# Retention feeding a channel mix on one core: the same words in a new written order

## The chip, the cores and the metric

The kernel runs on one core of a Trainium2 chip. A core has a matrix engine (TensorE, PE in the profile, with its weight loads as PEld), VectorE (DVE), ScalarE (ACT), GpSimd (POOL, which here only issues loads) and SyncE (SP, which here issues loads and stores). Each works through its own instructions in their written order, and waits on semaphores for the others. PSUM, which takes what PE computes, has eight banks of 512 f32 in each partition. The metric is the device time of one execution in microseconds.

## The reference

Inputs: q, k, v of 4 batches x 8 heads x 768 tokens x 64, two mixing vectors, and weights w_k (512 x 1024), w_v (1024 x 512), w_r (512 x 512), all f32. The output is 4 x 768 x 512 f32.

```python
gamma = 1.0 - 2.0 ** (-5.0 - np.arange(H))
for t in range(S):
    state = gamma * state + outer(k[:, :, t], v[:, :, t])
    y[:, :, t] = (1 / sqrt(D)) * (q[:, :, t] @ state)
x = y with the heads side by side            # batch, token, 512
xk = mu_k * x + (1 - mu_k) * x_prev          # x_prev: the token before
xr = mu_r * x + (1 - mu_r) * x_prev
out = sigmoid(xr @ w_r) * (maximum(xk @ w_k, 0) ** 2 @ w_v)
```

## The kernel before

The 4 x 768 tokens are cut into 12 blocks n of 256 tokens, three to a batch. Within a block the retention is computed in parallel: scores of k against q, masked, times v, plus what the carried state gives; between blocks of a batch the state is carried. Each block then goes through the channel mix. Some blocks are mixed in pairs (GROUPS, line 19: 3 with 4, 6 with 7, 9 with 10). Block 0 is loaded and transposed in two halves of heads.

What is issued, and in which order on every engine, is a written list of words, ORDER (lines 23 to 75). The loop in lines 720 to 734 reads it from the front, and each word calls one function (CODES, line 709), which issues that word's instructions. So the order on each engine is the order of its words in the list. A word is a code, its numbers (the first is nearly always the block n), an engine after ~ where that is open (v DVE, a ACT, p POOL, s SP), and after @ the PSUM bank or pair of banks. Waits between engines come from the data, the buffers and the banks that words share. The words:

| word | what it does | engine, line |
|---|---|---|
| lq, lk, lv | load q, k, v of a block; numbers behind n: a range of head pairs; two loads for k and v of a block from 1 on | POOL or SP, 223 to 238 |
| cq, ck | f32 to f16 of the halves of block 0 that SP loaded into k2s | ACT, 246 |
| wk.h, wv.h, wr | load halves of w_k, w_v; w_r | POOL, 698 to 707 |
| Tq, Tk then Eq, Ek | transposes; their copies out of PSUM | PE 265; ACT 286, 298 |
| vs | v times its decay | DVE 253 |
| S then M | scores; causal mask | PE 313, 325; DVE 346 |
| C, U, G | products for the state; their sums; decay to the next block | PE 360, 374; DVE or ACT 407, 422 |
| I, J, Y | carried state times q, and masked scores times v | PE 433 to 496 |
| D, dx | scaled result into xT; its difference to the token before | DVE 502, 526 |
| X.n.w.j | mix, w = 0 for xk and 1 for xr, j one of four parts; n is the first of its group | DVE 535 |
| K.n.g, Qa, Qb | xk @ w_k, part g; relu; square into k2s | PE 548; ACT 569, 574 |
| R.n.tb, s | xr @ w_r for half tb of the block; sigmoid | PE 589; ACT 598 |
| V.n.tb.half, O, st | product with w_v in two halves; times the sigmoid; store | PE 603; DVE 610; SP 616 |
| Vc, Oc, sc | the same for the last 128 tokens, in two column halves | PE 620; DVE 628; SP or ACT 635 |
| z.c | products of zeros on PE, whose results nobody reads: c // 4 products of f32 and c % 4 of f16, 512 columns each | PE 665 |
| mu, mt, me | load, transpose and copy the mixing vectors | ACT 653, PE 659, ACT 662 |
| gy | powers of the decay | DVE or ACT 681 |

K needs all four X of its block or group with w = 0, R all four with w = 1. Buffers are rings: four each for q, k, v as loaded (Q16, K16, V32), the sigmoids (RS) and the outputs (OS, two a block); three for vs, the transposed q and k, the mixes (XM) and the squares (k2s, whose second and third parts also take the first loads by SP, line 216); two for dx. A word that writes a bank waits until the words that read its last content are done.

The loop that reads the list:

```python
for word in ORDER.split():
    word, _, at = word.partition("@")
    word, _, eng = word.partition("~")
    code, *args = word.split(".")
    ...
    CODES[code](ENG.get(eng), *args)
```

Of the kernel before, what the change touches and what calls it, by code (L numbers as in the profile page):

```python
# [36 lines left out]
Eq.4~a wv.0~p K.2.2@2 Qa.2.2 M.3.1~v K.2.0@3 Qa.2.0 G.3~a M.3.0~v K.2.3@1 vs.4~v Qb.0.3 S.4.1@45
S.4.0@67 M.4.0~v I.3@23 M.4.1~v Qa.2.3 lq.6~p lq.7~p K.2.1@0 Qb.2.0 Y.3 C.4@67 V.1.0.0@1 U.4.0
U.4.1 G.4~a I.4@45 J.3 Qa.2.1 D.3~v dx.3~v Y.4 V.1.1.0@6 Tq.7@23 J.4 D.4~v wv.1~p Qb.2.1
V.0.1.0@0 lk.6~p V.0.0.0@7 X.2.1.2 dx.4~v X.3.0.1 X.3.0.2 X.3.0.3 Eq.7~a V.1.1.1 X.3.0.0 V.0.0.1  # L40
O.0.0 Tk.6@45 Ek.6~a lq.5~p Tq.6@23 lv.5~p Qb.2.2 V.0.1.1 Eq.6~a V.1.0.1 O.1.0 K.3.6@4 K.3.1@5
Qb.2.3 lk.5~p K.3.0@7 Qa.3.6 Tq.5@4 Qa.3.1 Qa.3.0 vs.5~v C.5@5 X.2.1.1 Eq.5~a Tk.5@1 Ek.5~a
S.6@23 O.0.1 O.1.1 lk.7~p U.5.0 Tk.7@67 Ek.7~a X.2.1.0 I.5@45 M.6~v X.3.1.3 K.3.2@0 K.3.3@1
Qa.3.2 Qb.3.1 lv.6~p S.5.0@23 Qa.3.3 Qb.3.0 X.3.1.1 S.5.1@67 Qb.3.3 X.2.1.3 Qb.3.2 K.3.4@0
st.0.0 Qa.3.4 M.5.1~v lk.8~p K.3.5@1 Qa.3.5 R.2.1@6 lv.8~p lk.9~p s.2.1 M.5.0~v Y.5 S.7@23
Tk.8@01 Ek.8~a J.5 X.3.1.0 X.3.1.2 R.3.1@7 s.3.1 V.2.0.0@6 K.3.7@0 lv.7~p vs.6~v R.2.0@7 V.2.0.1
D.5~v M.7~v s.2.0 dx.5~v X.5.1.1 O.2.0 Qa.3.7 Qb.3.6 V.2.1.0@1 Tk.9@23 C.6@45 U.6.0~a Ek.9~a
lq.8~p Tq.8@67 Qb.3.7 X.5.0.3 V.2.1.1 vs.7~v R.4.0@0 Eq.8~a U.6.1 U.6.2 X.5.0.0 U.6.3 st.0.1
R.3.0@2 C.7@45 X.5.0.1 s.4.0 I.6@67 s.3.0 st.1.1 X.5.0.2 K.5.3@3 Qa.5.3 O.2.1 lq.10~p K.5.1@0
Qa.5.1 G.6~v X.5.1.3 V.3.0.0@1 U.7.0 U.7.1 U.7.2 st.2.1 I.7@23 Y.6 vs.8~v U.7.3 G.7~a lq.11~p  # L50
R.4.1@0 D.6~v V.4.1.0@4 lv.11~p C.8@67 Y.7 V.3.1.0@5 Qb.5.1 Qb.3.4 Qb.3.5 V.3.0.1 dx.6~v s.4.1
U.8.0 U.8.1 V.3.1.1 Qb.5.3 D.7~v U.8.2 V.4.1.1 dx.7~v X.6.0.1 X.6.0.3 V.4.0.0@7 K.5.0@6 X.5.1.2
X.6.0.2 Qa.5.0 V.4.0.1 Qb.5.0 K.5.2@0 X.6.0.0 Qa.5.2 Qb.5.2 X.6.1.2 lv.9~p K.6.7@6 Qa.6.7 st.2.0
st.1.0 O.4.1 O.3.0 K.6.0@2 Qa.6.0 lk.10~p O.4.0 O.3.1 st.3.1 K.6.4@0 S.8@67 I.8@23 Tk.10@45
Qa.6.4 K.6.1@1 Ek.10~a X.6.1.1 X.5.1.0 Qa.6.1 Qb.6.1 K.6.6@0 Qb.6.0 Qa.6.6 vs.9~v K.6.5@4 Qa.6.5
M.8~v R.5.1@1 Qb.6.6 Tq.10@67 Eq.10~a s.5.1 Y.8 Tq.11@45 Qb.6.7 lv.10~p vs.10~v X.6.1.3 Eq.11~a
D.8~v dx.8~v lq.9~p X.8.0.2 X.8.0.1 lk.11~p R.5.0@0 s.5.0 K.6.3@6 Qa.6.3 V.5.1.0@7 Tq.9@23
X.6.1.0 Eq.9~a S.10@45 M.10~v Qb.6.3 C.9@01 U.9.0~v st.3.0 U.9.1 V.5.1.1 K.6.2@6 Qa.6.2 R.6.1@2
s.6.1 U.9.2 R.6.0@3 s.6.0 I.9@45 U.9.3 O.5.1 X.8.0.3 S.9@01 M.9~v X.8.0.0 G.9~a C.10@67 U.10.0
U.10.1 Qb.6.2 vs.11~v R.7.1@2 s.7.1 V.5.0.0@3 Qb.6.5 st.4.1 Tk.11@01 Ek.11~a U.10.2 U.10.3  # L60
V.5.0.1 Qb.6.4 K.8.0@2 Qa.8.0 G.10~v I.10@01 Y.9 C.11@67 st.4.0 R.7.0@2 O.5.0 V.6.1.0@3 D.9~v
U.11.0 U.11.1 s.7.0 K.8.3@4 Qa.8.3 V.6.1.1 U.11.2 I.11@67 st.5.0 dx.9~v O.6.1 S.11@45 X.8.1.2
Y.10 V.7.1.0@2 M.11~v D.10~v dx.10~v X.9.0.3 X.9.0.2 X.9.0.1 V.7.0.0@3 Y.11 X.9.0.0 Qb.8.0
# [12 lines left out]


# [687 lines left out]
```

## Time and profile before

| what | us |
|---|---|
| time, median of 3 runs | 156.48 (156.37 to 156.81) |
| the profiled execution's own time | 156.1 |
| its span, first to last instruction | 154.3 |
| PE busy / weight loads busy | 147.3 / 84.2 |
| DVE busy | 128.1 |
| ACT busy | 99.1 |
| POOL busy (issuing loads) | 55.2 |
| granted TensorE clock | 1.000 |

Between the profiled span and the time lie 1.8 us that no instruction covers. A busy share is the share of the span in which an engine had an instruction; matmuls overlap one another and are drawn longer than the distance at which they follow, so PE's share is an upper bound. A group's row gives the line, the engine, the operation, output and inputs by their names, the shape, the count, the busy time, the mean duration, and the idle time before it with what ended it. The lists below speak of words: since each engine runs its words in written order and the number of instructions of each word is known, the instructions of the timeline can be counted off against the list.

### The profile page before, as it was taken

The page shows a single profiled execution, that of the slowest core. Times are in us where ns is not written, and L with a number is a line of the kernel's source. Part 1 is how long each engine was busy: PE and PEld are TensorE (multiplying, and loading weights), DVE is VectorE, ACT ScalarE, POOL GpSimd, SP SyncE. Part 2 cuts the span into 40 slices and gives each one's busy share as a digit, 9 for nine tenths or more (in the row PEclk, how much of TensorE's full clock was granted, in tenths as well). Part 3 has the DMA queues.
Part 4 walks back from the last instruction along what each step waited for, and adds up shares of the span by engine and source line. Part 5 has one row for each costly group of instructions (what it writes and reads, how often), then busy time and mean ns, then how long its engine had stood idle before and what let it go on. Part 6 is the DMA issues. An engine that isn't in the chain of part 4 may idle for free.

```text
span 154.3 us, 5316 instructions
## 1 busy us (share of the span) xinstructions
PE 147.3 (95%) x2316; PEld 84.2 (55%) x2316; DVE 128.1 (83%) x203; ACT 99.1 (64%) x182; POOL 55.2 (36%) x67
## 2 busy tenths in 40 slices
...
DVE  2499999989999999999999999999999996050531
...
GB/s 140 283 184 171 204 243 248 166 216 207 190 180 216 219 293 267 188 78 88 305 248 175 12 272 8 0 6 4 138 4 4 0 68 204 0 20 53 155 117 204
DMA packets 44903, 22.29 MB, mean 144 GB/s; under 512 B 36424, under 2 KB 40400, under 8 KB 44880
## 3 DMA queue, kind: packets, MB, share of 16 engines
...
## 4 chain that ended last, share of the span: by engine, by line
PE 42%; DVE 36%; issue 8%; POOL 6%; DMA 5%; ACT 3%; DVEq 0%; POOLq 0%
PE ps L605 13%; PE ps L553 9%; PE ps L593 8%; DVE xk L539 6%; PE ps L563 5%; DVE dx L530 5%; DMA q<-in_q_dram 5%; DVE xr L539 4%; DVE a L355 4%; DVE xT L515 3%; DVE vs L254 3%; DVE tg L420 3%; DVE os L611 2%; POOL k L231 2%; DVE xT L508 2%
## 5 line engine op out<-in xcount | busy, mean ns | idle before, releaser
L605 PE MATMUL ps<-wv,k2s 128*128 128x512 f16 x184 | 44.4, 380 | 0.0
L572 ACT ACTIVATE kr<-ps 128x512 f32<-128x512 f32 x48 | 27.8, 597 | 21.2 <-PE ps L563 11.7
L605 PEld LDWEIGHTS <-k2s 128*128 128x128 f16 x184 | 17.3, 98 | 18.8
L611 DVE SCALAR_TENSOR_TENSOR os<-ps,rs 128x512 f32<-128x512 f32 x23 | 15.1, 684 | 14.4 <-PE ps L605 7.9
L593 PE MATMUL ps<-wr,xr 128*128 128x512 f16 x96 | 23.9, 380 | 0.0
L231 POOL DMA_DIRECT2D v<-in_v_dram x22 | 19.8, 916 | 10.5 <-DVE vs L254 7.9
L563 PE MATMUL ps<-xk,wk 128*128 128x256 f16 x192 | 23.5, 273 | 0.0
L231 POOL DMA_DIRECT2D k<-in_k_dram x22 | 19.6, 905 | 10.5 <-DMA wk<-in_moe_w_k_dram 3.4
L553 PE MATMUL ps<-xk,wk 128*128 128x512 f16 x96 | 22.6, 379 | 0.8 <-DVE xk L539 0.8
L599 ACT ACTIVATE rs<-ps 128x512 f32<-128x512 f32 x24 | 14.1, 602 | 13.5 <-PE ps L593 9.4
L563 PEld LDWEIGHTS <-wk 128*128 128x128 f16 x192 | 18.2, 98 | 4.6 <-DMA wk<-in_moe_w_k_dram 0.5
L539 DVE SCALAR_TENSOR_TENSOR xr<-dx,mu,xT 128x256 f16<-128x256 f32 (+1 forms) x36 | 19.3, 566 | 0.0
L539 DVE SCALAR_TENSOR_TENSOR xk<-dx,mu,xT 128x256 f16<-128x256 f32 (+1 forms) x36 | 18.8, 567 | 0.2
L254 DVE TENSOR_TENSOR vs<-v,csm_sb 128x1024 f16<-128x1024 f32 x12 | 14.6, 1216 | 2.1 <-DMA v<-in_v_dram 2.1
L553 PEld LDWEIGHTS <-wk 128*128 128x128 f16 x96 | 9.0, 98 | 12.1 <-DVE xk L539 1.1
L242 ACT COPY kT<-ps 128x1024 f16<-128x1024 f16 (+1 forms) x13 | 12.2, 951 | 4.4 <-PE ps L279 3.3
L584 ACT ACTIVATE k2s<-kr 128x512 f16<-128x512 f32 x24 | 14.8, 632 | 0.2
L530 DVE TENSOR_TENSOR dx<-xT 128x1024 f32<-128x1024 f32 x12 | 14.6, 1219 | 0.2
L580 ACT ACTIVATE k2s<-kr 128x512 f16<-128x512 f32 x24 | 14.7, 629 | 0.1
L355 DVE TENSOR_TENSOR a<-ps,c_sb 128x1024 f16<-128x1024 f32 (+1 forms) x14 | 14.4, 1062 | 0.0
L242 ACT COPY qT<-ps 128x1024 f16<-128x1024 f16 (+1 forms) x13 | 12.3, 954 | 3.2 <-PE ps L273 2.9
L593 PEld LDWEIGHTS <-xr 128*128 128x128 f16 x96 | 8.7, 98 | 9.7
(67 smaller groups left out, 154.3 us busy)
## 6 DMA issues: line engine op xcount, KB each, us to landing
...
wk<-in_moe_w_k_dram POOLq DMA_DIRECT2D x2, 512.0 KB, 10.2
wv<-in_moe_w_v_dram POOLq DMA_DIRECT2D x2, 512.0 KB, 10.0
...
```

Source lines behind the costliest of these rows:

```text
L231: e.dma_start(out=dst[:, :, i * D : i * D + D], in_=src[:, i * P : i * P + P].rearrange("h p d -> p h d"),)
L242: e.copy(out=out, in_=in_)
L254: e.tensor_tensor(out=VS(n), in0=V32(n).rearrange("p h (i d) -> p i h d", i=2), in1=gks[:, int(half(n) or wide(n)), :, :, None].to_broadca ...
L355: nc.vector.tensor_tensor(out=a_full(n)[:, i, :, j0:j1], in0=pairs(banks("S", n, i, j0))[:, :, j0:j1], in1=(below if wide(n) else causal[: ...
L530: e.tensor_tensor(out=DX(k)[:, :, m * TM + t0 : m * TM + t1], in0=x[:, :, c + t0 : c + t1], in1=x[:, :, c - 1 + t0 : c - 1 + t1], op=ALU.s ...
L539: nc.vector.scalar_tensor_tensor(out=XM[w](k)[:, j, t0:t1], in0=DX(k)[:, j, t0:t1], scalar=mu[:, w * NCO + j : w * NCO + j + 1], in1=x[:, ...
L553: nc.tensor.matmul(banks("K", n, g), lhsT=wk16[:, co, g * P : g * P + P], rhs=XM[0](k)[:, co, :], start=(co == 0), stop=(co == NCO - 1),)
L563: nc.tensor.matmul(pz[:, i, :], lhsT=wk16[:, co, fo * P : fo * P + P], rhs=XM[0](k)[:, co, m * TM + t0 : m * TM + t1], start=(i == 0 and c ...
L572: nc.scalar.activation(out=kr, in_=banks("K", n, g, *u), func=AF.Relu)
L593: nc.tensor.matmul(banks("R", n, tb), lhsT=XM[1](k)[:, co, t : t + P], rhs=wr16[:, co, :], start=(co == 0), stop=(co == NCO - 1),)
L605: nc.tensor.matmul(banks("V", n, tb), lhsT=K2(n)[:, fo, tb * P : tb * P + P], rhs=wv16[:, fo, :], start=(fo == 0), stop=(fo == NFO - 1),)
L611: nc.vector.scalar_tensor_tensor(out=OS(2 * n + tb), in0=banks("V", n, tb), scalar=1.0 / (KSC * KSC), in1=RS(2 * n + tb), op0=ALU.mult, op ...
```

## The change

Only ORDER changes. After it, each word but z stands in the list once as before, with the same engine; the positions differ on all engines, and so do many banks behind @. Of z the counts and places are new: before 12, 2, 2, 4, 1, 4, 1, 1, 2, after 12, 1, 3, 3, 2, 3, 5, 11. At the beginning, lk.0.2.4 and lq.0.2.4 (POOL) stand ahead of lv.0 and are the first to be transposed, ahead of the halves that SP loads, and of those lq.0.0.2 now comes ahead of lk.0.0.2; lv.4, wv.0 and wv.1 stand further ahead among the loads. The last V words, the last two Vc and their stores change places: sc.11.1.1 on ACT is the last.

```diff
@@ -21,57 +21,57 @@
 ORDER = """
-lk.0.0.2~s gy.0 lq.0.2.4~p lv.0~p lq.0.0.2~s lk.0.2.4~p ck.0.0.2~a z.12@6 Tk.0.0.2@0 mu
-Tq.0.2.4@1 cq.0.0.2~a z.2@6 Tq.0.0.2@2 Ek.0.0.2~a vs.0~v Eq.0.0.2~a z.2@6 S.0.1.0.2@45
-S.0.0.0.2@67 M.0.0.0.2~v Eq.0.2.4~a M.0.1.0.2~v Tk.0.2.4@2 Ek.0.2.4~a C.0@01 U.0.0~a U.0.1
-S.0.0.2.4@67 M.0.0.2.4~v I.0@45 S.0.1.2.4@01 mt@3 me M.0.1.2.4~v lv.1~p vs.1~v gy.1~a G.0~a
-z.4@2 Y.0 D.0~v lk.1~p Tk.1@0 Ek.1~a C.1@67 U.1.0 lq.1~p z.1@2 Tq.1@1 Eq.1~a dx.0~v X.0.0.0
-z.4@2 S.1.1@01 lk.2~p I.1@45 S.1.0@23 M.1.1~v M.1.0~v lq.2~p Tq.2@6 Eq.2~a wk.1~p X.0.0.3 Tk.2@0
-X.0.0.2 z.1@1 Y.1 J.1 X.0.0.1 D.1~v U.1.1 Ek.2~a z.1@2 S.2.1@01 S.2.0@23 K.0.2@6 dx.1~v K.0.3@4
-Qa.0.3 Qa.0.2 wk.0~p z.2@5 K.0.1@7 Qa.0.1 K.0.0@5 Qb.0.2 X.0.1.0 X.1.0.2 lv.2~p Qa.0.0 Qb.0.1
-X.1.0.3 wr~p X.1.0.1 X.1.0.0 K.1.2@4 lv.3~p G.1~a K.1.1@7 X.0.1.1 vs.2~v Qa.1.2 Qb.1.2 M.2.1~v
-Qb.0.0 C.2@5 U.2.0 K.1.0@6 lq.3~p Qa.1.1 X.0.1.2 X.0.1.3 K.1.3@0 Qa.1.3 I.2@45 R.0.1@1 R.0.0@7
-s.0.1 M.2.0~v Y.2 Qa.1.0 X.1.1.3 X.1.1.2 Qb.1.0 Tq.3@1 Eq.3~a J.2 X.1.1.0 X.1.1.1 R.1.0@6 s.0.0
-lk.3~p Tk.3@1 vs.3~v D.2~v dx.2~v X.2.0.2 X.2.0.0 C.3@23 X.2.0.3 Ek.3~a s.1.0 X.2.0.1 lk.4~p
-U.3.0~a R.1.1@0 lq.4~p s.1.1 Tk.4@1 S.3.1@45 S.3.0@67 Qb.1.1 Qb.1.3 U.3.1 lv.4~p Tq.4@0 Ek.4~a
...
-K.8.2@4 Qa.8.2 X.8.1.0 X.9.1.1 K.8.1@5 Qa.8.1 D.11~v V.6.0.0@0 V.7.0.1 V.6.0.1 K.9.3@1 K.9.7@5
-Qa.9.7 X.8.1.1 V.7.1.1 X.8.1.3 dx.11~v K.9.2@4 O.7.0 Qb.8.1 Qb.9.7 O.6.0 Qa.9.3 st.5.1 Qa.9.2
-X.11.1.0 Qb.8.3 X.11.0.3 K.9.1@5 K.9.4@6 st.7.0 Qa.9.1 Qb.9.1 R.8.0@1 s.8.0 V.8.1.0@3 Qb.9.2
-X.9.1.0 K.9.0@0 Qa.9.0 Qb.8.2 X.9.1.2 Qb.9.3 K.9.6@1 Qa.9.6 Qb.9.6 O.7.1 st.7.1 K.9.5@7 Qa.9.5
-V.8.0.0@0 X.11.0.2 X.11.0.1 Qb.9.0 X.11.0.0 K.11.3@2 K.11.0@1 Qa.11.3 st.6.1 R.8.1@5 V.8.1.1
...
-s.10.0 V.9.0.0@7 V.9.1.0@0 Qa.11.1 Qb.11.1 O.8.1 Qb.9.5 Qb.11.3 Qa.11.0 st.8.1 K.11.2@6 Qa.11.2
-V.10.1.0@5 Qb.11.2 Qb.11.0 V.9.1.1 R.9.0@1 X.11.1.3 s.9.0 X.11.1.1 V.9.0.1 O.9.0 st.9.0
-V.11.0.0@6 s.10.1 s.9.1 O.9.1 st.9.1 V.10.0.0@1 V.10.1.1 O.10.1 st.8.0 st.10.1 V.11.0.1 R.11.0@0
-s.11.0 O.11.0 V.10.0.1 R.11.1@7 s.11.1 O.10.0 st.10.0 Vc.11.1.1@0 Oc.11.1.1 Vc.11.1.0@6 st.11.0
-sc.11.1.1~a Oc.11.1.0 sc.11.1.0~s
+gy.0 lk.0.2.4~p z.12@7 Tk.0.2.4@0 lq.0.2.4~p z.1@1 Tq.0.2.4@1 lv.0~p lv.1~p lk.1~p mu lq.1~p
+lq.2~p lk.2~p wk.1~p wk.0~p lv.2~p wr~p Ek.0.2.4~a lv.3~p lk.3~p lq.3~p lq.0.0.2~s Eq.0.2.4~a
+z.3@2 S.0.1.2.4@23 lk.0.0.2~s M.0.1.2.4~v S.0.0.2.4@45 cq.0.0.2~a ck.0.0.2~a Tq.0.0.2@1
+Eq.0.0.2~a Tk.0.0.2@0 Ek.0.0.2~a vs.0~v M.0.0.2.4~v z.3@6 S.0.1.0.2@67 M.0.1.0.2~v C.0@23
+U.0.0~a U.0.1 z.2@1 I.0@01 gy.1~a S.0.0.0.2@45 lk.4~p lq.4~p M.0.0.0.2~v z.3@6 Y.0 Tk.1@4 vs.1~v
+C.1@67 D.0~v G.0~a U.1.0 Ek.1~a dx.0~v U.1.1 mt@5 me Tq.1@3 Eq.1~a z.5@2 S.1.1@01 I.1@45
+S.1.0@23 X.0.0.2 M.1.1~v M.1.0~v z.11@6 Y.1 J.1 Tq.2@2 X.0.0.3 X.0.0.0 X.0.0.1 K.0.3@3 Eq.2~a
+Qa.0.3 D.1~v lv.4~p X.0.1.2 dx.1~v X.0.1.0 Tk.2@0 Ek.2~a G.1~a K.0.2@2 Qa.0.2 K.0.0@3 K.0.1@0
+Qa.0.0 Qb.0.0 X.1.0.3 S.2.0@67 Qa.0.1 X.1.0.2 S.2.1@45 X.1.0.1 X.1.0.0 K.1.3@3 Qa.1.3 vs.2~v
+C.2@2 X.0.1.3 X.1.1.2 U.2.0 X.0.1.1 K.1.0@0 I.2@23 wv.0~p Qb.0.3 Qa.1.0 Qb.0.2 K.1.1@1 Qa.1.1
+M.2.0~v R.0.0@0 M.2.1~v Qb.1.0 s.0.0 R.0.1@1 Qb.1.1 Y.2 X.1.1.1 J.2 X.1.1.3 s.0.1 Qb.0.1 X.1.1.0
+Tk.3@0 Ek.3~a R.1.0@1 s.1.0 Tq.3@4 Eq.3~a vs.3~v C.3@67 D.2~v K.1.2@0 Qa.1.2 R.1.1@2 s.1.1
+S.3.1@45 U.3.0~a dx.2~v X.2.0.3 X.2.0.2 X.2.0.0 X.2.0.1 Qb.1.3 wv.1~p S.3.0@01 M.3.0~v Tk.4@3
+M.3.1~v lq.7~p X.2.1.1 Ek.4~a K.2.0@2 Qa.2.0 U.3.1 Tq.4@6 Qb.1.2 Eq.4~a K.2.3@3 Qa.2.3 K.2.2@4
+vs.4~v S.4.1@01 M.4.1~v S.4.0@67 M.4.0~v lk.6~p lq.6~p K.2.1@5 I.3@23 Qa.2.2 G.3~a Qa.2.1 Qb.2.1
+Y.3 C.4@01 V.1.1.0@5 V.0.1.0@4 X.2.1.2 U.4.0 I.4@67 U.4.1 J.3 X.2.1.3 Qb.2.0 Qb.2.3 Y.4 D.3~v
+X.2.1.0 lv.5~p dx.3~v V.0.0.0@1 V.0.0.1 O.0.0 Tq.7@23 J.4 D.4~v dx.4~v X.3.0.0 X.3.0.2 X.3.0.3
+V.1.0.0@0 V.1.0.1 Qb.2.2 Eq.7~a G.4~a V.2.0.0@1 V.2.0.1 Tk.6@23 Tq.6@67 Eq.6~a Ek.6~a V.0.1.1
+lk.5~p X.3.0.1 V.1.1.1 O.0.1 K.3.1@6 O.1.1 K.3.4@7 Qa.3.1 lq.5~p S.6@23 Qb.3.1 Qa.3.4 lk.8~p
+vs.5~v lv.6~p Tk.5@6 Ek.5~a O.1.0 M.6~v X.3.1.1 X.3.1.2 Tq.5@5 Eq.5~a C.5@0 K.3.6@7 U.5.0
+K.3.2@6 Qa.3.6 S.5.0@23 M.5.0~v S.5.1@45 M.5.1~v R.2.0@7 vs.6~v K.3.0@0 Qa.3.2 Qb.3.6 s.2.0
+I.5@23 lk.7~p st.0.1 Tk.8@67 Ek.8~a Y.5 V.2.1.0@4 st.1.0 K.3.5@5 X.3.1.0 Qa.3.0 Tk.7@67 J.5
+Qa.3.5 X.3.1.3 K.3.3@0 Ek.7~a R.3.1@5 Qb.3.0 Qa.3.3 C.6@67 st.0.0 O.2.0 s.3.1 lk.9~p U.6.0~a
+lv.7~p D.5~v dx.5~v X.5.0.0 X.5.0.1 lv.9~p lv.8~p X.5.0.3 Tk.9@23 S.7@01 Ek.9~a U.6.1 U.6.2
+V.2.1.1 X.5.0.2 R.2.1@5 s.2.1 Qb.3.5 K.3.7@2 Qb.3.3 vs.7~v K.5.0@5 Qa.5.0 Qb.3.4 R.3.0@3 U.6.3
+M.7~v s.3.0 K.5.1@5 C.7@67 G.6~v I.6@01 Qa.3.7 Qb.3.7 O.2.1 U.7.0 lq.11~p lq.8~p Qb.5.0 U.7.1
+R.4.1@3 s.4.1 U.7.2 K.5.2@4 Qa.5.2 U.7.3 I.7@23 Qb.3.2 vs.8~v Y.6 D.6~v st.1.1 K.5.3@7 Qa.5.3
+V.4.0.0@4 C.8@67 Tq.8@01 dx.6~v Qa.5.1 Y.7 D.7~v dx.7~v X.6.0.3 X.6.0.2 Eq.8~a V.4.0.1 X.6.0.0
+V.3.1.0@5 Qb.5.2 V.3.0.0@2 V.3.0.1 O.3.0 V.3.1.1 G.7~a U.8.0 st.2.1 X.6.0.1 Qb.5.1 R.4.0@3 s.4.0
+U.8.1 lq.10~p O.3.1 lk.10~p lk.11~p V.4.1.0@0 V.4.1.1 K.6.0@1 st.2.0 O.4.1 Qa.6.0 U.8.2 X.5.1.1
+K.6.1@5 Qa.6.1 K.6.4@1 I.8@23 O.4.0 st.4.0 Qa.6.4 Tk.10@67 Qb.5.3 S.8@45 st.3.0 X.5.1.0 Ek.10~a
+lv.10~p lq.9~p Qb.6.0 K.6.7@0 Qa.6.7 V.5.1.0@1 Tq.11@67 X.6.1.2 M.8~v Tq.10@45 Y.8 V.5.1.1
+Eq.10~a X.5.1.3 Qb.6.7 X.5.1.2 Eq.11~a vs.9~v D.8~v K.6.6@0 Qa.6.6 Tq.9@45 C.9@23 X.6.1.1 Eq.9~a
+Qb.6.1 dx.8~v S.10@67 M.10~v U.9.0~v K.6.2@0 K.6.5@4 Qa.6.2 st.3.1 X.8.1.3 Qb.6.2 U.9.1 lv.11~p
+X.8.1.1 Qb.6.4 Qa.6.5 K.6.3@5 Qa.6.3 Qb.6.3 U.9.2 vs.10~v R.5.1@0 X.8.0.0 R.5.0@6 s.5.1 s.5.0
+U.9.3 V.5.0.0@5 V.5.0.1 X.6.1.3 Qb.6.5 O.5.0 V.7.0.0@0 O.5.1 st.5.1 V.6.0.0@6 st.5.0 X.6.1.0
+Qb.6.6 X.8.0.3 I.9@23 G.9~a S.9@45 M.9~v V.7.0.1 vs.11~v R.7.0@1 s.7.0 R.6.1@7 s.6.1 C.10@45
+X.8.0.1 X.8.1.2 st.4.1 Y.9 U.10.0 U.10.1 D.9~v X.8.0.2 R.6.0@1 s.6.0 O.7.0 V.6.1.0@7 V.6.1.1
+U.10.2 U.10.3 G.10~v O.6.1 st.6.1 K.8.1@2 Qa.8.1 Qb.8.1 V.6.0.1 O.6.0 st.6.0 C.11@01 I.10@45
+X.8.1.0 Tk.11@23 Ek.11~a U.11.0 K.8.2@7 K.8.0@6 Qa.8.2 U.11.1 Qa.8.0 S.11@23 U.11.2 I.11@01 Y.10
+M.11~v st.7.0 dx.9~v K.8.3@6 D.10~v dx.10~v X.9.1.2 X.9.0.2 R.7.1@7 X.9.0.0 X.9.0.3 Qa.8.3
+Qb.8.3 V.7.1.0@6 X.9.0.1 V.7.1.1 Qb.8.0 V.8.1.0@4 V.8.0.0@5 R.8.0@2 Y.11 D.11~v Qb.8.2 V.8.1.1
+s.7.1 V.8.0.1 K.9.1@7 K.9.0@3 Qa.9.0 K.9.7@0 R.8.1@3 s.8.0 K.9.2@2 K.9.5@1 s.8.1 K.9.3@3 Qb.9.0
+Qa.9.7 Qa.9.1 Qa.9.3 Qb.9.3 Qa.9.2 Qb.9.2 X.9.1.0 Qb.9.1 X.9.1.3 K.9.4@7 Qa.9.4 Qa.9.5 dx.11~v
+X.11.0.3 X.11.1.1 X.11.0.0 X.11.0.2 X.11.1.3 K.9.6@3 X.11.0.1 K.11.2@0 Qa.9.6 K.11.0@2 X.11.1.0
+X.11.1.2 Qb.9.6 Qa.11.2 Qb.11.2 O.8.1 st.8.1 V.9.1.0@4 K.11.1@7 R.11.0@3 Qb.9.7 Qa.11.1 Qb.11.1
+O.7.1 V.9.0.0@0 X.9.1.1 R.10.1@1 st.7.1 R.9.0@7 R.11.1@6 Qb.9.4 Qb.9.5 V.9.1.1 Qa.11.0 R.9.1@2
+V.9.0.1 s.9.1 s.10.1 Qb.11.0 O.8.0 st.8.0 s.9.0 V.10.1.0@2 O.9.1 s.11.1 K.11.3@1 Qa.11.3 Qb.11.3
+V.10.1.1 V.10.0.0@1 O.9.0 st.9.0 s.11.0 O.10.1 st.9.1 R.10.0@0 s.10.0 V.11.0.0@3 st.10.1
+V.10.0.1 O.10.0 st.10.0 V.11.0.1 O.11.0 st.11.0 Vc.11.1.0@0 Oc.11.1.0 sc.11.1.0~s Vc.11.1.1@1
+Oc.11.1.1 sc.11.1.1~a
 """
```

28 lines of the change are left out of this document (removed).

## The prediction

> **What bounds the kernel now.** I read the page first: busy shares and the slices.
>
> ```profile
> span 154.3 us, 5316 instructions
> PE 147.3 (95%) x2316; PEld 84.2 (55%) x2316; DVE 128.1 (83%) x203; ACT 99.1 (64%) x182; POOL 55.2 (36%) x67
> DVE  2499999989999999999999999999999996050531
> ```
>
> PE and DVE are both nearly full, DVE only up to slice 33 (127 us). The busy times by stage separate the stretches:
>
> ```profile
> 16.00:50.00 34.00, 33.09 (x551) 22.11 (x552) 33.18 (x47) 24.16 (x47) 21.67 (x26) 1.00 1.55 208
> 50.00:85.00 35.00, 34.70 (x628) 19.07 (x627) 34.48 (x55) 24.38 (x43) 19.44 (x22) 1.00 1.36 206
> 85.00:119.00 34.00, 33.24 (x762) 18.67 (x761) 33.00 (x52) 22.07 (x39) 0.00 (x0) 1.00 0.15 51
> 119.00:151.00 32.00, 32.00 (x172) 16.73 (x171) 16.41 (x29) 18.85 (x35) 0.00 (x0) 1.00 0.21 80
> ```
>
> Columns: window, its length, then PE, PEld, DVE, ACT, POOL busy (instructions), clock, DMA share, GB/s. From 16 to 119 DVE is 97 to 98% busy; from 119 on PE alone is. PE's busy time is flattered: a 128x512 matmul is drawn 0.38 us long, but eight of them start within 1.72 us. So I read start to start. The timeline around the hand-over:
>
> ```profile
> 116.20 2.74 DVE L539 SCALAR_TENSOR_TENSOR xk<-dx,mu,xT 128x512 f16<-128x512 f32 x4
> 119.00 1.89 PE L553 MATMUL ps<-xk,wk 128*128 128x512 f16 x8 [0.40 <-DVE xk L539]
> 120.72 1.03 PE L605 MATMUL ps<-wv,k2s 128*128 128x512 f16 x4
> ```
>
> K.9.3 starts 0.06 us after the last of DVE's four X.9.0 words: DVE set the pace until here. The start-up is set by loads:
>
> ```profile
> 1.05 4.84 PE L668 MATMUL ps<-zero 128*128 128x512 f32 x6 [1.05 <-DVE xT L651]
> 5.82 0.41 PE L273 MATMUL ps<-c_sb,k 128*64 128x128 f16 x8
> 7.76 1.22 DVE L254 TENSOR_TENSOR vs<-v,csm_sb 128x1024 f16<-128x1024 f32 x1 [2.10 <-DMA v<-in_v_dram]
> 17.24 0.64 PE L273 MATMUL ps<-c_sb,q 128*64 128x128 f16 x16 [0.70 <-DMA q<-in_q_dram]
> 22.79 3.28 PEld L563 LDWEIGHTS <-wk 128*128 128x128 f16 x31 [0.48 <-DMA wk<-in_moe_w_k_dram]
> ```
>
> **Two queue sums.** Both engines work through a fixed list, so I add each list up with start-to-start times: K, R, V 0.865 us a word (eight matmuls in 1.72); T 0.47 or, for n from 6, 0.27; S 0.23 to 0.26; C 0.12 to 0.45; I, J 0.13 to 0.24; Y 0.4 to 0.7; on DVE vs, M and D 1.14, dx 1.2, a single X 0.395, a paired one 0.66, U 0.34 (0.45 when the next U reads it), O 0.60, the two D instructions of a late block 1.49. A word's start less the sum ahead of it is the time that its engine has lost so far. Before, PE's list adds up to 145.0. It has lost 3.46 at K.1.0 (26.64 us), 6.01 at K.9.3 (119.00), 6.0 at the end: 145.0 + 6.0 = 151.0, where the last Vc is done. DVE's list (130.8) shows 5.3 at D.0 (12.86 us) and 4.9 at O.7.1 (126.87): it never waited between, and my DVE prices are 0.4% high. So 2.4 us of PE's loss is the start beyond 1.05, and 2.55 is waiting for DVE.
>
> **The change, part by part.**
>
> Every word but z is there on both sides, with the same engine and shape. Loads, stores, casts and activations cost what they did; their order counts.
>
> *Zeros.* Units after: 12, 1, 3, 3, 2, 3, 5, 11 = 40; before: 12, 2, 2, 4, 1, 4, 1, 1, 2 = 29. The first 12 stand alike ahead of the first transpose. The other 28 against 17 cost 0.216 each (a quarter of 0.865): +2.4 us on PE's list. Hidden only where PE would have waited.
>
> *Switches.* PE pays where a word of 128x128 weights meets one of smaller tiles. The weight loads show it:
>
> ```profile
> 45.34 3.14 PEld L605 LDWEIGHTS <-k2s 128*128 128x128 f16 x16
> 48.90 0.33 PEld L279 LDWEIGHTS <-k 64*64 64x64 f16 x32 [0.42 <-issue]
> 48.90 0.45 PE L279 MATMUL ps<-c_sb,k 64*64 64x64 f16 x32
> ```
>
> Among big words a load runs ahead of its matmul; at a switch both start together, the word before lasts 0.95 instead of 0.86, and on the way back a small word lasts 0.11 longer. Counted in the written order from the first K word on: 26 pairs before, 29 after: 3 x 0.2 = +0.6 us. [...]
>
> PE's list after: 145.0 + 2.4 + 0.6 = 148.0. DVE's: 130.5 (fewer words that need their neighbour).
>
> *Start.* Before, the first heads of k and q come by SP into k2s and are cast first. After, POOL's lk.0.2.4 and lq.0.2.4 are used first; SP's halves are cast later; lv.0 is third on POOL instead of second. POOL's first load landed at 5.9 (issue 1.24 plus 4.6 in the list of issues), the second, twice as large, at 7.7 (vs.0 starts at 7.76), a third of 128 KB 0.6 later. So lk at 5.8, lq near 6.5 (no row shows a small second load; between 6.3 and 7.7, the size of the third is nearest), lv.0 at 8.35. From there a serial chain: Tq to 6.95, Eq (0.59) to 7.6, cq and ck (0.52 to 0.62 each) to 8.65, Tk, Ek.0.0.2 to 9.7, S.0.1.0.2, its mask, C.0, U.0.0 on ACT to 10.9, U.0.1 to 11.45, M.0.0.0.2 to 12.2, then DVE in its written order without a gap: vs.1, D.0 (to 14.7, before 14.1), U.1.0, dx.0, U.1.1, X.0.0.2, M.1.1, M.1.0 to 19.15. Y.1 starts at 19.2; the PE list ahead of it is 17.55, so PE has lost 1.65. z.11 ends within 0.2 us of M.1.0: it fills that wait. K.0.0 comes at 22.9, wk.0 landed at 22.75, since the queue has moved the same bytes by then; lq.2 (second now, lk.2 behind it) lands by 16 and is wanted at 19.9; lv.2, wr, lv.3 stand as before. lk.3 now precedes lq.3: 31.1 against 31.2 wanted. The first loss is 1.65 where before it was 3.46: -1.8.
>
> *Middle.* I laid the two lists beside each other and looked at every place where one engine needs the other. Before, PE lags and only waits. After, the lists are locked: DVE waits for PE at D.3 (0.3), D.5 (0.3) and M.11 (0.4), PE for DVE at C.2, K.2.0, Y.5, Tq.8 and V.3.0.0 (0.1 to 0.15 each) and K.8.1 (0.35; behind X.8.0.2, which stands after D.9). Sum for PE 1.1 with my DVE prices, 0.95 with the 0.4% off. At K.9 PE is already later than X.9.0.1, so the 0.56 of before goes. -2.55 + 0.95 = -1.6.
>
> *Bank reuse with one word between* (K.5.0 and K.5.1, K.6.0 and K.6.4, K.8.3 and V.7.1.0, K.9.0 and R.8.1, R.9.1 and V.10.1.0, K.11.3 and V.10.0.0): ACT needs 0.26 + 0.60 + 0.05 = 0.91 to clear a bank, the word between gives 0.865. Bounds 0 (ACT runs ahead) and 0.5 a place (it is one activation behind); nearest is 0.05 on some, +0.2 in all.
>
> *Moved loads and stores.* POOL's queue lands one load after another to about 65 us in both orders. wv.0 and wv.1 come ahead of lq.7, lk.6, lq.6: about 40 and 42, lq.7 43.6, wanted at 43, 46 and 47. lk.9 waits for C.5 (57), lk.11 for C.7 (73); what stands behind them on POOL (lv.7 to lv.8; lv.10, lq.9, lv.11) is wanted 8 us later or more. On SP, st.0.0 goes behind st.0.1 and st.1.0: it would land near 62, O.2.0 wants its buffer at 64. Cost 0, up to 2 if stores are later than 5.5 us, the slowest of before. The last store is on ACT instead of SP: issue 0.38 against 0.33, landing not shown; 0 to 0.3, taken as 0.
>
> Sum: +2.4 +0.6 -1.8 -1.6 +0.2 = -0.2. The profiled execution spans 154.3 and took 156.1; it becomes 154.1 and 155.9. The median is 156.48, 0.4 above the profiled run, so on the medians 156.3.
>
> **The rivals.** *The start comes late (slower).* If lq.0.2.4 lands at 7.7 like the second load of before, every step up to M.1.0 is 1.2 later, and nothing behind it absorbs that, because DVE is shifted with PE. 156.3 + 1.2 = 157.5. It decides from a landing of 7.2 on (+0.7). For it: the second load's row, and that SP's transfers were in use at 4.0 and 5.3. Against: half the bytes.
> *Locked lists cost more (slower).* PE and DVE pass each other within 0.2 us at some 14 gates, and ACT at 6; 0.1 more at each is +2 less what is shared: 157.4. For it: before, one engine led and only one waited. Against: the same prices reproduce before to 0.1 us at its end.
> *The gates are loose (faster).* If DVE's words run at their shortest rows and ACT is ahead, the 0.95 and 0.2 vanish: 155.2.
> *The zeros are too long* (a gap is shorter than its zeros): z.11 alone is 2.4, so a M.1.0 that is ready 1 us early gains nothing; this would turn a good start into no change, and is held in the first case.
>
> **How the numbers follow.** Lists cancel, 156.3, own range 155.7 to 156.9: 0.42 (of it faster 0.12, same 0.21, slower 0.09). Late start 0.22, slower. Locked lists 0.14 (slower 0.11, same 0.03). Loose gates 0.22, faster. About 0.3% (0.47 us) is what a measurement of this kernel can tell from no change. Faster 0.34, same 0.24, slower 0.42. The range takes in both slower rivals' prices with their spread and the faster one's: 155.0 to 158.0.
>
> **What would show it.** First Q transpose at 6.55 and Eq.0.2.4 by 7.6; D.0 done at 14.7; Y.1 at 19.2 right behind z.11; K.0.0 at 22.9 without a wait for wk; K.8.1 waiting for xk; DVE with small waits for PE at D.3, D.5, M.11; K.9.1 without a wait, near 123.9; the last Vc starting near 149.9. Wrong if transposes wait for q beyond 7.2, if PE waits for ACT by more than 0.5 in all, or if a load or store is late in the middle.

## The result, and the profile after

The changed kernel takes 157.99 us in the median of 8 runs (157.13 to 158.45), the kernel before 156.44 (156.17 to 156.99, 8 runs on the same chip). The ratio is 1.0084, with a 95% interval from 1.0056 to 1.0113: slower, by 1.5 us, where no change was forecast. The profiled execution of the changed kernel spans 156.4 us and took 158.22; before it was 154.3 and 156.1, so the two profiles differ by 2.1. 157.99 lies just inside the range of 155.0 to 158.0.

The page of the changed kernel, its head and the row of VectorE in the slices:

```profile
span 156.4 us, 5324 instructions
PE 149.9 (96%) x2325; PEld 84.7 (54%) x2325; DVE 128.4 (82%) x203; ACT 99.1 (63%) x182; POOL 55.0 (35%) x67
DVE  1479999999989999999789889999989999700431
```

VectorE, which stood at 9 from slice 3 to 33 before but for one 8, now has slices of 7 and 8 from 74 us on. The busy times by stage, in the same windows as before (window, length, PE, PEld, DVE, ACT, POOL, clock, DMA share, GB/s), point there too:

```profile
16.00:50.00 34.00, 33.84 (x496) 22.00 (x495) 33.09 (x49) 24.46 (x47) 21.81 (x26) 1.00 1.57 210
50.00:85.00 35.00, 33.09 (x682) 18.77 (x681) 33.14 (x46) 24.88 (x45) 18.68 (x22) 1.00 1.39 206
```

Between 50 and 85 us PE, otherwise busy all the time, is idle for 1.9 us. PE's waits (what it waited for, us in total, times, longest) say what for:

```profile
PE ps L668 <- DVE xT L651: 1.1, 1, 1.1
PE ps L442 <- issue: 1.0, 1, 1.0
PE ps L605 <- issue: 0.9, 1, 0.9
PE ps L332 <- issue: 0.2, 1, 0.2
```

The waits for xk, q, a and vs of before are gone, as forecast. In their place stand two for "issue", that is, for nothing that the profile shows. The timeline of PE gives the places, with the weight loads and VectorE's words beside the second:

```profile
76.42 0.27 PE L442 MATMUL ps<-qT,tg 64*64 64x64 f16 x8
77.66 0.25 PE L442 MATMUL ps<-qT,tg 64*64 64x64 f16 x4 [0.97 <-issue]
...
80.75 1.90 PE L605 MATMUL ps<-wv,k2s 128*128 128x512 f16 x8
83.58 1.24 PE L605 MATMUL ps<-wv,k2s 128*128 128x512 f16 x5 [0.93 <-issue]
```

```profile
80.75 1.62 PEld L605 LDWEIGHTS <-k2s 128*128 128x128 f16 x9
```

```profile
80.92 1.51 DVE L508 TENSOR_TENSOR xT<-ps,gy_sb 128x512 f32<-128x512 f32 x2 [0.25 <-PE ps L442]
```

The first lies in the middle of a word. Y.6 ends with twelve matmuls of L442; eight ran, the last starting at 76.49, and the other four came from 77.66 on. Inside a word nothing new is waited for, neither data nor a bank. The second lies at the beginning of V.3.0.0. The eight matmuls in the row at 80.75 are V.4.0.1 and V.3.1.0, the last starting at 82.27; the nine weight loads show that the first one of V.3.0.0 had been issued too, and its four matmuls came from 83.58 on. So the expectations below, which speak of a stop inside V.3.0.0, mean the place between its first weight load and its first matmul. There a wait could stand, but none that the profile shows comes late enough: V.3.0.0 reads the same weights as V.3.1.0 just ahead of it and the other half of the same squares, and its bank 2 was last read by the first of the two instructions of D.7, which was over when the second began at 81.74 (in the run with loads cut, below, V.3.0.0 starts at 80.83, before D.7's second instruction is done at 81.00). Counted against the queue sum of the prediction, PE loses 1.20 at the first place and 1.09 at the second, 2.3 together. That is more than the whole difference between the two kernels.

What is special about the places shows when PE's instructions (matmuls, weight loads and the few records of its sequencer, in the order of their start) are counted: 2497 stand ahead of the first stop and 2753 ahead of the second, 256 more, and 449 ahead of a smaller one of 0.23 at the beginning of S.1.0 (L332), eight times 256 before. The page lists a DMA queue of 18 packets and 0.29 MB named "instruction", that is 16 KB each, and PE has 4650 matmuls and weight loads, 18 times 256 and a little. So I read it as PE's own instructions, brought in pieces of 256. The page counts this queue's packets (0.8%) and those of the queue of POOL's loads (74.8%, 54.9% in the run with loads cut, below) as shares of the same 16 DMA engines' time. The transfers' own times, from the records of that queue, set beside PE's passing of the borders (the last column is the time between the starts of the two matmuls at the border, where it is out of the ordinary):

| kernel, border | PE passed the border before | transfer begins, lasts | PE goes on | 256 took | stood still |
|---|---|---|---|---|---|
| before, 2241 | 62.3 | 66.25, 0.97 | 68.6 | 6.3 | 0 |
| before, 2497 | 68.6 | 69.78, 1.32 | 75.15 | 6.5 | 0 |
| after, 2241 | 65.3 | 68.54, 1.35 | 71.35 | 6.1 | 0 |
| after, 2497 | 71.35 | 75.35, 0.97 | 77.66 | 6.3 | 1.16 |
| after, 2753 | 77.66 | 80.72, 1.30 | 83.58 | 5.9 | 1.31 |

A transfer begins 1 to 4 us after PE has passed the border before its own, and where PE stands, it goes on 1.3 to 1.6 us after the transfer's end. Set side by side in this way, the transfers and borders of all 18 profiles of this case (306 pairs) hold none that PE passed sooner than 1.24 us after its transfer's end. So this is the theory: while loads run, 256 instructions of PE cannot take less than some 6 us. The change has Y.6, C.8, Tq.8 and Y.7 (the small tiles, 48 to 96 instructions in 0.2 to 0.6 us) close together, and would run 256 in some 5 us there.

### The profile page after: what moved, and what is told of

The parts are those of the page before. It is cut to its first block, busy times and chain, and to the rows that moved or that the text cites. A ratio compares the mean times of both kernels' runs of the same rounds, so it can differ in the third digit from the quotient of the medians.

```text
span 156.4 us, 5324 instructions
## 1 busy us (share of the span) xinstructions
PE 149.9 (96%) x2325; PEld 84.7 (54%) x2325; DVE 128.4 (82%) x203; ACT 99.1 (63%) x182; POOL 55.0 (35%) x67
## 2 busy tenths in 40 slices
DMA packets 44903, 22.29 MB, mean 142 GB/s; under 512 B 36424, under 2 KB 40400, under 8 KB 44880
## 3 DMA queue, kind: packets, MB, share of 16 engines
q0 software_dynamic: 39920, 14.95, 74.8%
## 4 chain that ended last, share of the span: by engine, by line
PE 93%; DVE 3%; issue 2%
PE ps L605 26%; PE ps L563 14%; PE ps L593 14%; PE ps L553 14%; PE ps L668 5%; PE ps L273 4%; PE ps L442 3%; PE ps L279 2%; PE ps L332 2%; PE ps L479 2%; DVE a L355 1%; PE ps L367 1%; PE ps L675 1%; PE ps L319 1%; PE ps L623 1%
## 5 line engine op out<-in xcount | busy, mean ns | idle before, releaser
L605 PE MATMUL ps<-wv,k2s 128*128 128x512 f16 x184 | 43.7, 380 | 0.9 <-issue 0.9
L563 PE MATMUL ps<-xk,wk 128*128 128x256 f16 x192 | 24.2, 273 | 0.0
(67 smaller groups left out, 157.4 us busy)
```

The costliest lines, as they stand in the source:

```text
L563: nc.tensor.matmul(pz[:, i, :], lhsT=wk16[:, co, fo * P : fo * P + P], rhs=XM[0](k)[:, co, m * TM + t0 : m * TM + t1], start=(i == 0 and c ...
L605: nc.tensor.matmul(banks("V", n, tb), lhsT=K2(n)[:, fo, tb * P : tb * P + P], rhs=wv16[:, fo, :], start=(fo == 0), stop=(fo == NFO - 1),)
```

## Experiments: are late instructions the cause?

**The loads cut.** The same order on all engines, with less for the DMA engines to carry (18.16 MB instead of 22.29; from 70 to 76 us a DMA share of 0.25 instead of 1.89):

```diff
             hs = slice(2 * j0, 2 * j1)
+            if e is nc.gpsimd and (n > 7 or (x is v and n == 7)):
+                hs = slice(0, 1)
             src = x[b, hs, t0 : t0 + TM, :]
```

> The changed kernel, but the loads of k and q from block 8 on and of v from block 7 on bring only the first of eight heads, so the transfers of POOL all but stop from 61 us on; the output of these blocks is not the reference's. Instruction order is the same. Theory 'PE runs out of instructions' (its instructions come in pieces of 256 through the same transfer engines, and a piece comes 4 us late while loads run): the two places where PE stood still with nothing waited for (inside Y.6 at 76.5 us, 1.2; inside V.3.0.0 at 82.3 us, 1.3) vanish or shrink below 0.3 each, the pieces' transfers start within 1.5 us of the border before, and the time falls by 2.3 from 158.0 to about 155.7 (155.2 to 156.3). Rival 'the words or their banks': both stalls stay, 158.0 within 0.4. Rival 'all of the miss is the late start': no change either.

Measured 155.58 us (155.31 to 155.63), 0.9927 of the kernel before (0.9899 to 0.9955), 2.4 less than the changed kernel. PE's whole list of waits is now

```profile
PE ps L670 <- DVE xT L653: 1.1, 1, 1.1
PE ps L334 <- issue: 0.2, 1, 0.2
```

and the timeline where Y.6 had stopped (L444 is L442 above, two lines of edit further down):

```profile
75.94 0.31 PE L444 MATMUL ps<-qT,tg 64*64 64x64 f16 x12
```

Y.6's twelve matmuls now run through, V.3.0.0 too. The pieces' transfers begin at 70.13 and 77.22, 0.7 before and 1.2 after PE passes the border before them; the 256 instructions took 5.2 and 4.8 us. So the order itself is faster than that of before by 0.9 us.

**The same cut in the kernel before**, as a control:

> The kernel before with the same loads cut to one head of eight (k and q from block 8 on, v from block 7 on); its output for these blocks is not the reference's. Theory 'PE runs out of instructions': the order before has no stall at any border of 256 instructions, so nothing is won: 156.5 within 0.4. Rival 'cutting loads makes any order faster, by whatever it is that transfers hold up': it falls as the changed kernel did, by about 2.4, to 154.1.

156.44 us, ratio 1.0000 (0.9956 to 1.0044). Cutting loads as such wins nothing; it wins what late instructions cost.

**Loads added**, in the changed kernel and in the one before, behind POOL's last load:

```diff
+lv.8~p lk.8~p lq.8~p lv.8~p lk.8~p lq.8~p lv.8~p lk.8~p lq.8~p lv.8~p lk.8~p lq.8~p
```

> The changed kernel with twelve loads added behind POOL's last one: lv.8, lk.8, lq.8 four times over, into buffers whose content has been used, so that the transfers go on from 86 to about 108 us instead of ending there. The result is the same. Theory 'PE runs out of instructions while loads run': new stalls with nothing waited for appear where 256 instructions take less than 6 us in that stretch: about 3 us at the border that PE reached at 97.1 (Tq.9, 3.0 us after the one before) and up to 1.2 us at the one at 110.7 (4.8 us after its own); none between 86 and 94; time 160.5 to 162.5. Rival 'loads do not touch PE, POOL is off the path': 158.0 within 0.5, no stall but the two known ones.

> The kernel before with twelve loads added behind POOL's last one (lv.8, lk.8, lq.8 four times, into buffers already used up), so that transfers go on from about 85 to 103 us. The result is the same. Theory 'PE runs out of instructions while loads run': the borders at 96.7, 101.4 and 106.5 us, reached 3.8, 4.7 and 5.1 us after the ones before them, now stall by 1 to 2, 0.1 to 1 and 0 to 1 us with nothing waited for; part of it is slack that PE had against VectorE; 157.2 to 159.5. Rival 'the order before is safe, loads are off the path': 156.5 within 0.4.

The changed kernel took 158.89 in one run, 0.9 more than its median and less than the 160.5 to 162.5 that were expected. The stop at the border near 97 came (timeline of the changed kernel with loads, inside Tq.9):

```profile
95.84 0.29 PE L278 MATMUL ps<-c_sb,q 64*64 64x64 f16 x12
97.75 0.35 PE L278 MATMUL ps<-c_sb,q 64*64 64x64 f16 x20 [1.62 <-issue]
```

The one forecast near 110 did not: its transfer began at 106.43, as PE passed the border before, although loads still ran. How long a piece is held up varies: in this profile the two old stops cost only 0.3 and 0.2 beyond the ordinary distance of two matmuls, and a new one of 1.1 stood at 71.7. That is why the time rose less than forecast, and it fits the wide spread of the changed kernel's runs (157.13 to 158.45). The kernel before rose to 158.37 (ratio 1.0104, 1.0063 to 1.0146), with stops it never had (inside a transpose and inside a Y):

```profile
98.03 0.38 PE L278 MATMUL ps<-c_sb,q 64*64 64x64 f16 x22 [0.88 <-issue]
...
109.05 0.37 PE L462 MATMUL ps<-a,vs 64*64 64x64 f16 x22 [1.36 <-issue]
```

**The count shifted.** 124 more instructions ahead of all from Y.1 on:

```diff
-z.11@6
+z.9@6 p.64@6     (p: products of 64x64 zeros, 64 columns)
```

> The changed kernel with z.11 cut to z.9 and 64 products of 64x64 zeros behind it, which take about as long as the two units but put 124 more instructions ahead of everything from Y.1 on. All work is done. Theory 'PE runs out of instructions' with borders every 256: the stalls leave Y.6 and V.3.0.0; the border that lay in Y.6 now lies in K.5.2 (7.5 us after the one before it: no stall), and the next one at the end of Tq.8, only 3 us later, so there PE stands 2.5 to 3 us in the middle of Tq.8; time 158.0 to 159.2. Rival 'the words, their banks or a fixed time': the stalls stay in Y.6 and V.3.0.0 with 1.2 and 1.3.

158.13 us in one run. Y.6 and V.3.0.0 run through: the stops went with the count, not with the words. The big stop forecast in Tq.8 did not come, since that piece's transfer began 0.9 us after its border instead of 3. Instead there are three at other borders, 0.4, 0.5 and 0.8, where the loads are over and 256 instructions took only 3.4, 3.45 and 3.7 us:

```profile
117.49 0.28 PE L440 MATMUL ps<-qT,tg 64*64 64x64 f16 x10 [0.59 <-issue]
```

So without loads a piece that stopped PE took 3.4 to 3.7 us; at one border of the changed kernel (97.07) 256 instructions went through in 2.98 without a stop, since the transfer began 0.3 us after the border before. With loads, the stops so far stand at 4.8 to 7.1 us: not a fixed 6, but as late as the transfer begins. These five runs (the two that add loads to the changed kernel and shift the count are single runs) settle the cause: stops appear and vanish with the loads, in both orders, and move with the count of instructions.

## Experiments: which part of the change makes them late?

**The words spread out.** Between 74 and 90 us:

```diff
-R.4.1@3 s.4.1 U.7.2 K.5.2@4 Qa.5.2 U.7.3 I.7@23 ... Y.6 D.6~v ... K.5.3@7 ... V.4.0.0@4 C.8@67 Tq.8@01 ... Y.7 D.7~v
+R.4.1@3 s.4.1 R.4.0@2 s.4.0 U.7.2 K.5.2@4 Qa.5.2 U.7.3 K.5.3@7 I.7@23 ... Y.6 X.5.1.1 X.5.1.0 D.6~v ... V.4.0.0@4 V.4.0.1 V.3.0.0@0 ... Y.7 D.7~v
+... V.3.1.0@5 ... V.3.0.1 C.8@67 ... V.3.1.1 Tq.8@23
```

> The spread order again, with K.5.3 behind U.7.3 (in the first one K.5.3 overwrote bank 7 before U.7.3 had read it, which put a wait of its own on VectorE). All work is done. Theory 'PE runs out of instructions': in 70 to 90 us no stall above 0.4 with nothing waited for; new ordinary waits of up to 0.6 at D.7 and K.6.0 take some of the gain; 156.4 to 157.5 against 158.0 of the changed kernel. Rival 'the stalls belong to Y.6 and V.3.0.0': both stay, 158 or more.

157.66 us (ratio 1.0064, 1.0038 to 1.0090); a first try with K.5.3 ahead of U.7.3, so that U.7.3 waited for K.5.3 and summed its product instead of C.7's, took 158.93, where 156.2 to 157.5 was expected, with a stop of 0.8 at 71.65. In the profile of the second no stop is left between 70 and 90 us, and the stretches that take 5.2 and 4.8 us when nothing is late last 6.75 and 6.8. But against the queue sum PE loses 0.25 at K.6.1, 0.43 at Tk.10 and 0.20 at S.8, and the list is 0.4 longer by switches: what is won is nearly spent. The time is 0.2 above the range that was expected. The profiled execution was the fastest of the ten, 156.95, so the others may have had stops that it does not show; the same words with z.9 (below) had one of 0.8 at 71.7.

**A searched order.** All words of PE, VectorE and ScalarE from 57 to 101 us reordered by row prices, with 6.4 us or more to each 256 instructions:

```diff
-O.1.0 M.6~v X.3.1.1 ... U.9.2
+(the same words of PE, VectorE and ScalarE in another order; loads and stores as they were)
```

> The changed kernel with the words of PE, VectorE and ScalarE between O.1.0 and U.9.2 (57 to 101 us) in an order in which by row prices 256 PE instructions take 6.4 us or more wherever loads run and in which no new wait above 0.4 appears; all else, the start and the zeros too, as changed. All work is done. Theory 'PE runs out of instructions': most of the 2.4 us that the cut loads gave back are won without cutting them: 155.4 to 156.6, and no stall above 0.5 with nothing waited for. Rival 'cut loads helped in another way than by the instruction pieces': 157.5 to 158.5 as the changed kernel.

158.76 us (1.0127, 1.0087 to 1.0167): a miss. One stop, at a border where the changed kernel's profile has none:

```profile
69.69 0.88 PEld L561 LDWEIGHTS <-wk 128*128 128x128 f16 x9
72.30 0.75 PEld L561 LDWEIGHTS <-wk 128*128 128x128 f16 x7 [1.74 <-issue]
```

The piece's transfer began at 69.54, 4.9 after PE passed the border before. In eight profiles with the changed kernel's loads it began between 68.2 and 70.0, 3.2 to 5.3 after the border; with loads cut it began at 65.58, 0.9 after it. So 6.4 us was too cheap a price here.

**Only the loads moved.** lv.9, lq.11, lq.10 and lk.10 go behind lk.11, which POOL issues at 74.4:

```diff
-lv.9~p lv.8~p ... lq.11~p lq.8~p ... lq.10~p ... lk.10~p lk.11~p
+lv.8~p ... lq.8~p ... lk.11~p lk.10~p lq.10~p lq.11~p lv.9~p
```

> The changed kernel with four loads of POOL (lv.9, lq.11, lq.10, lk.10) moved behind lk.11, which POOL issues at 74.4 us since it waits for C.7. The order on all other engines is as changed. All work is done. Theory 'a piece of instructions waits in line behind the loads that POOL has issued ahead': the line is empty from about 70 to 76, so the piece wanted from 71.4 on comes before 74 and the stall inside Y.6 (1.2) vanishes; the one inside V.3.0.0 meets the moved loads and keeps 0.5 to 1.5; 156.6 to 157.4. Rival 'only the clustering of small words counts': both stalls stay, 158.0 within 0.4. Rival 'late loads cost': vs.9 or Tk.10 wait, 158 or more.

156.19 us (0.9986, 0.9962 to 1.0010): 1.8 less than the changed kernel, by four loads that nobody waits for, and less than the 156.6 to 157.4 that were expected. The stretch 70 to 76 us of the kernel before, the changed kernel and this one, in this order (the last but one column is the packets' time as a share of 16 DMA engines' time; at 1.89 packets overlap):

```profile
70.00:76.00 6.00, 6.00 (x135) 3.81 (x134) 5.83 (x14) 3.65 (x7) 5.89 (x7) 1.00 0.64 173
```

```profile
70.00:76.00 6.00, 6.00 (x81) 3.80 (x79) 5.78 (x12) 5.39 (x10) 1.71 (x3) 1.00 1.89 193
```

```profile
70.00:76.00 6.00, 6.00 (x112) 3.96 (x113) 5.81 (x11) 5.53 (x11) 1.88 (x3) 1.00 0.23 79
```

0.64, 1.89 and 0.23. With the line empty the piece's transfer began at 72.15 instead of 75.35, and Y.6 ran through; at V.3.0.0 0.14 is left, where 0.5 to 1.5 was expected.

**The load orders exchanged** between the two kernels, from lk.7 on (POOL's words alone, as they follow one another):

```diff
-lk.8~p lv.6~p lk.7~p lk.9~p lv.7~p lv.9~p lv.8~p lq.11~p lq.8~p lq.10~p lk.10~p lk.11~p lv.10~p lq.9~p lv.11~p
+lk.7~p lv.6~p lk.8~p lv.8~p lk.9~p lv.7~p lq.8~p lq.10~p lq.11~p lv.11~p lv.9~p lk.10~p lv.10~p lq.9~p lk.11~p
```

> The changed kernel with one part undone: POOL's loads from lk.7 on in the order of before (lk.7, lv.6, lk.8, lv.8, lk.9, lv.7, lq.8, lq.10, lq.11, lv.11, lv.9, lk.10, lv.10, lq.9, lk.11); every other engine as changed. All work is done. In that order POOL pauses before lv.11, which waits for vs.7 (71 us). Theory 'the change's load order is a cause': the line of transfers empties before 72, the piece of instructions for Y.6 comes 2 to 3 us sooner and that stall vanishes; 156.3 to 157.3 against 158.0. Rival 'clustered small words alone': 157.6 to 158.4.

> The kernel before with this one part of the change: POOL's loads behind lv.7 as the change has them (lv.9, lq.11, lq.8, lq.10, lk.10, lk.11, lv.10, lq.9, lv.11; lv.8 stays ahead of lk.9); every other engine as before. All work is done. Theory 'the load order alone makes pieces late': stalls of 0.3 to 1.5 at the border at 68.6 us (margin 1.4 before) or the one at 75.2, of which VectorE's lead hides nothing; 156.8 to 158.0 against 156.5. Rival 'it takes the clustered words too': before's 256 instructions take 6.3 us or more there, so 156.5 within 0.4.

The changed words with the loads of before: 157.20 (1.0035, 1.0006 to 1.0063). Y.6 ran through (transfer at 71.60), V.3.0.0 stopped for 1.7; the waits put that down to VectorE's dx, which V does not read (in the changed kernel V.3.0.0 went on at 83.58, before dx.7 was done at 83.69), and PE went on 1.40 after the transfer's end as at the other borders. The words of before with the changed loads: 156.80 (1.0012, 0.9982 to 1.0043), with no new stop at any border. That time is at the lower end of what the theory of the load order gave and within what its rival gave, and the one profile is of an execution of 159.52 in which the clock was at half from 10.9 to 17.7 us; so this half is weaker than the other. As far as it goes, it takes both: a piece that began 3.5 us after the border did not hurt words that took 7.98 us to 256 (to the border at 86.7 in that profile), and fast words did not stop where the line was empty.

## Experiments: the zeros

```diff
-z.11@6
+z.9@6
```

> The spread order, and z.11 cut to z.9 (two units of zeros, 0.43 us of PE, less ahead of Y.1). All work is done. Theory 'z.11 is longer than its gap' (in four profiles Y.1 starts 0.46 to 0.50 after M.1.0 has ended): Y.1 and all behind it come 0.4 earlier, 0.3 to 0.5 less than e5_spread. Rival 'PE is not the bound there, or VectorE sets the pace from 20 us on': no difference (within 0.15).

> e9_search with z.11 cut to z.9. All work is done. Theory 'z.11 is 0.46 us longer than its gap, and PE is the bound behind it': 0.3 to 0.5 less than e9_search. Rival 'VectorE sets the pace behind the start': the same within 0.15.

> e13_defer with z.11 cut to z.9. All work is done. If PE is the bound from Y.1 on: 0.3 to 0.5 less than e13_defer, 156.2 to 157.0. If not: the same within 0.15.

Three pairs, the shorter zeros always below: 157.66 and 156.98 for the spread order, 158.76 and 157.87 for the searched one, 156.19 and 155.80 for the moved loads. The two units are 0.43 us; the pairs differ by 0.4 to 0.9, more than that where stops vary as well. The last, 155.80 us, is 0.9937 of the kernel before (0.9897 to 0.9977): the changed order with four loads later and two units of zeros less beats both kernels. Its time is below the 156.2 to 157.0 that were expected, since the moved loads had already won more.

Spread words and moved loads together, with z.9:

> e6_spread_z9 (spread words, z.9) with the same four loads moved behind lk.11. All work is done. Theory 'pieces of instructions wait behind issued loads': the borders at 78 and 85 us have 6.5 and 6.8 us anyway, and the one at 71.4 to 72.1, which still stalled by 0.8 in one profile of that order, gets its piece sooner; 156.1 to 156.8, at most 0.4 above the kernel before. Rival 'the order between 74 and 90 us costs the rest by its own waits': 156.9 or more, no gain from moved loads.

156.66 us (1.0002, 0.9980 to 1.0023), 0.9 above the moved loads without the spreading. So with the loads moved the spread order wins nothing; what it costs fits its own waits and switches, which no run took apart.

The first zeros cut as well, on the searched order:

```diff
-z.12@7
+z.10@7
```

> e10_search_z9 with the first zeros cut from z.12 to z.10. All work is done. Theory 'the first zeros outlast the first load when the clock rises late' (profiles had it rise between 3.9 and 7.0 us; with 7.0 the first transpose started at 6.47, with 5.2 at 5.99, the load landed at 5.9): the first transpose starts at 5.9 to 6.0 in any case, and the median falls by 0 to 0.4 against e10_search_z9, the spread of the runs too. Rival 'less zeros let the clock fall or rise later, so the first blocks run slow': the same or up to 1 us slower.

158.06 us against 157.87: no difference that the runs can tell. In its profile the load of k landed late enough for PE to wait for it 1.1 us.

## Why the prediction was wrong, step by step

**The step that failed** is "Moved loads and stores ... Cost 0". It asked of each load whether its reader waits, and there it was right: in the waits of PE's matmuls and of VectorE no load stands behind the start. It did not ask who else uses the DMA engines. PE runs out of instructions where the loads hold up its next piece; with the loads cut the stops are gone and 2.4 us come back. That is more than the miss (157.99 against 156.3, 1.7): without the stops the kernel is 0.7 faster than forecast. None of the rivals had this cost. That 157.99 still lies inside the range, and that slower had the largest chance, is luck: the range's upper end and most of that chance stood there for the late landing of q and for the locked lists, and neither came. "POOL's queue lands one load after another to about 65 us in both orders" was also read too coarsely. The DMA row of the slices, 3.9 us each, first before, then after:

```profile
DMA  4999999999999999973999170000300015001435
```

```profile
DMA  4999999999999979999997050005041000310324
```

Before, the line runs thin in the 18th and 19th slice (66 to 73 us), where the change now puts its fast words; after, it is full from 59 to 82 us.

**The queue sums** held. In the profile with loads cut PE's list ends with a loss of 2.38 on 148.0; forecast was 148.0 + 2.8. By its profile the span is 153.8 against a forecast of 154.1, the time 155.58 against 156.3, the last Vc starts at 149.50 against 149.9, and K.9.1 at 123.55 against 123.9. The forecast was a good one of a kernel that gets its instructions in time.

**Zeros, +2.4**: right in the list. "z.11 ends within 0.2 us of M.1.0" was wrong: it ends 0.5 behind. The changed kernel, VectorE with M.1.1 and M.1.0, then PE with z.11, Y.1:

```profile
17.21 2.34 DVE L355 TENSOR_TENSOR a<-ps,c_sb 128x1024 f16<-128x1024 f32 x2
```

```profile
17.50 1.98 PE L668 MATMUL ps<-zero 128*128 128x512 f32 x4
19.32 0.81 PE L675 MATMUL ps<-zero 128*128 128x512 f16 x3
20.07 0.64 PE L479 MATMUL ps<-a,vs 128*64 128x128 f16 x16
```

M.1.0 is done at 19.55, and Y.1 starts at 20.07, behind the zeros. The rival "zeros too long" was there, but was put into the first case without a price.

**Start, -1.8**: the loads came as said (k at 5.89, q at 6.65; the rival "late start" decided from 7.2). But Y.1 came at 20.07 instead of 19.2, with a loss of 2.51 instead of 1.65. The steps: the first Q transpose 7.36 instead of 6.55, Eq.0.2.4 done 8.40 instead of 7.6, D.0 15.10 instead of 14.7.

```profile
1.05 5.49 PE L668 MATMUL ps<-zero 128*128 128x512 f32 x6 [1.05 <-DVE xT L651]
6.47 0.63 PE L273 MATMUL ps<-c_sb,k 128*64 128x128 f16 x8
```

The six records of the first zeros end at 6.54 here and at 5.89 before, and the eight transposes behind them take 0.63 against 0.41. The trace's record of the full clock begins at 6.97 here and at 5.11 before. In the profile with loads cut it begins at 5.22, the Q transpose at 6.76, Y.1 at 19.50. In three more profiles with the changed start (the loads of before, the searched order, the added loads) it begins at 4.8 to 5.3, and Y.1 comes at 19.24 to 19.31, nearly as forecast; in two with an early clock in which PE waited 0.5 and 0.8 for the load of k it comes at 19.82 and 19.62. So the moment at which the clock rises goes with some 0.5 us at the start; the prediction had taken the one profile's moment for fixed. K.0.0 did not wait for wk, as forecast (23.87 instead of 22.9, late by the same).

**Middle, 0.95**: with loads cut it is 0.4 (2.38 less 1.95 at Y.1). VectorE's waits at D.3 (0.50) and M.11 (0.51) came, D.5's was 0.1; K.8.1 did not wait for xk: it starts 0.08 after X.8.0.2 has ended, right behind the word ahead of it. **Bank reuse, +0.2**: nothing; PE waits for ScalarE nowhere in the list of waits. **Switches, +0.6**: not tried apart; the list with them gives the end to 0.4. Of the rivals, "loose gates" was the nearest: with loads cut, 0.7 of its 1.15 came true, hidden in the changed kernel under the stops. "Locked lists" did not occur.
